# Ten pairs of token tiles in seven block products instead of eight, in the second projection of an attention-and-MLP kernel

## The chip, the cores and the metric

The kernel runs on one core of a Trainium2 chip. A core has five engines with instruction queues of their own: TensorE (PE: matrix products, into PSUM), VectorE (DVE), ScalarE (ACT: activations and copies), GpSimd (POOL), and SyncE (SP), which here only issues DMAs. They meet through semaphores. SBUF is the working memory; PSUM has eight banks of 512 fp32 columns, into which TensorE accumulates and which VectorE and ScalarE read. The metric is device time in microseconds, the median of the runs.

## The reference

Four batches of eight heads, 768 positions, head size 64; every query sees the first four positions and a window of 128. The attention output, as 3072 tokens of 512 features, goes through two projections with a gate between them.

```python
scores = q @ k^T / sqrt(64)          # keep: position < 4, or 0 <= row - column < 128
a = softmax(where(keep, scores, -1e9))
x = (a @ v) as (3072, 512)
h = x @ w_in                         # (512, 2048)
g = h * (1 / (1 + exp(-beta * h)))   # beta: one number per column
out = g @ w_out                      # (2048, 512), fp32
```

## The kernel before

**Blocks.** The tokens are cut into eight blocks of 384 (half a batch each; `hb` in the attention part, `T_` in the projections). A block is three token tiles of 128. For each block the kernel loads q, k and v (`load`, 256 KB each, into fp32 staging buffers `stg`, two slots per name), casts them to bf16 (`cast`), brings q and k into a transposed layout (`T` on TensorE for blocks 0 to 2, `XP` with DMA transposes issued by SyncE from block 3, `CUT`, on), computes scores in bursts of up to three tiles (`SC`, `band`, `SS`), takes exponentials on ScalarE, masks on GpSimd and VectorE, multiplies by v (`AV`), normalises on VectorE and transposes the result into `xT` (`OT`, again DMA transposes from block 3 on).

**First projection.** `HQ(T_, m)` makes one of the sixteen groups of 128 hidden features of a block: four 384-column matmuls (line 1023) into one bank, a tanh on ScalarE (line 1028), and `(t + 1) * h` on VectorE (line 1030) into `g`, bf16. That is twice the gated value, so a factor 0.5 is left for the output. There are three `g` buffers.

**Second projection.** `OQ(T_, t, j)` is a quarter of one token tile: four matmuls with a 128x128 piece of `g` as the stationary operand and 512 columns of `w_out16` as the moving one (line 1046). After the fourth quarter the bank is copied to `osb` with the factor 0.5 (`copies`, on ScalarE line 524 or VectorE line 530) and stored (line 1064). The very last tile is done in two parts of 384 and 128 columns.

**Who sets the order.** Nothing loops at run time. `later` is a string, written out by hand, of one letter per step (T, S, A, R, H, O); each letter takes the next step of its kind. `background` puts loads, casts and DMA transposes in between by their estimated times. Every operation is recorded in `Graph` with its reads and writes; `any_of` gives a choice of engines. `arrange` then orders the operations of every engine by estimated ready times (it may move a group of matmuls a few places) and keeps GpSimd and some VectorE operations apart (`lock`). Each engine runs its list in order; `resolve` turns dependences into semaphore waits.

Of the kernel before, what the change touches and what calls it, by code (L numbers as in the profile page):

```python
# [4 lines left out]
BF16 = mybir.dt.bfloat16  # L5
# [22 lines left out]
class Graph:  # L28
# [15 lines left out]
    def __init__(self):  # L44
        self.ops = []
        self.writers = {}
        self.readers = {}
        self.last_x = {}
        self.free = {e: 800.0 for e in self.ENGINES}
        self.dma_free = 2500.0  # L50
        self.stalls = [(16000.0, 1100.0), (34000.0, 700.0)]
        self.port = {"gp": 0.0, "dve": 0.0}
        self.group = 0
        self.filler, self.fill_to = None, 0
# [5 lines left out]
    def add(self, eng, fn, ns=0, r=(), w=(), x=(), dma=None, alts=None, after=(), hold=550, chain=None, lock=False):  # L60
# [31 lines left out]
        at = self.free[eng]  # L92
        for p, _ in deps:
            at = max(at, p.end + (0 if p.eng == eng and not p.dma else self.HOP))
        self.place(o, at)
        self.ops.append(o)
        return o

# [296 lines left out]

def _program(nc, G, sb, ps, q, k, v, w_in, w_out, beta, out):
# [49 lines left out]
    BAND, KW = 8, 64  # L446
    LANES, QUADS = [6,7], [3,5,7]
# [5 lines left out]
    def any_of(alts, r=(), w=(), x=(), lock=False):  # L453

        return G.add(min(alts, key=lambda e: G.free[e] + alts[e][1]), None, 0, r, w, x, None, alts, lock=lock)
# [134 lines left out]

    def load(hb, n, i):

        b, t0, z = hb // 2, hb % 2 * HALF, hb % NSTG
# [10 lines left out]
        after = [("stg", n, z, j) for j in range(4)] if hb in range(CUT, CUT + NSTG) and n != "v" else ()  # L604
# [20 lines left out]
    def cast_w(j):  # L625
# [13 lines left out]
        any_of(copies(dst, src_, {"act": 947} if j in W0 else {"gp": 1060} if j < 4 else {"act": 947, "dve": 602, "gp": 1060}), r=[("wst", j % NWS)], w=[("w16", m, h)], lock=True)  # L639

    def cast(hb, n, i):

        z = hb % NSTG
# [371 lines left out]
    def HQ(T_, m):  # L1015
# [6 lines left out]
        for c in range(4):  # L1022
# [4 lines left out]
        spare_ = [("wst", NWS // 2 + z) for z in range(NWS // 2)] if (T_, m) == (NG - 1, 0) else []  # L1027
        add("act", lambda e: e.activation(tt[ti][:, :], hp, AF.Tanh, bias=0.0, scale=hbeta[:, m:m + 1]),  # L1028
            act_ns(HALF) + 93, r=["hbeta"], w=[("t", ti)], x=[("B", bs[0])])
        add("dve", lambda e: e.scalar_tensor_tensor(gt[T_ % NG][:, m, :], tt[ti][:, :], 1.0, hp, ALU.add, ALU.mult),  # L1030
            dve_ns(HALF), r=[("t", ti)], w=[("g", T_, m)] + spare_, x=[("B", bs[0])])
# [5 lines left out]
    def OQ(T_, t, j):  # L1037
# [7 lines left out]
        for m in range(4 * j, 4 * j + 4):  # L1045
# [3 lines left out]
                r=[("w16", 4 + m // 4, m // 2 % 2), ("g", T_, m)], x=[("B", bk)])  # L1049
        if j == 3 and n < NOUT:  # L1050
            z = os_i[0] % NOS
            os_i[0] += 1
            add("act", lambda e: e.activation(osb[z][:, 0:n], P[:, bk, 0:n], AF.Copy, bias=0.0, scale=0.5),
# [4 lines left out]
        elif j == 3:  # L1058
            z = os_i[0] % NOS
            os_i[0] += 1  # L1060
            any_of(copies(osb[z][:, :], P[:, bk, :], {"dve": 608, "act": 493}, 0.5), w=[("osb", z)], x=[("B", bk)])
# [6 lines left out]


# [15 lines left out]
    OS += [(T_, t, j) for T_ in range(1, NSB) for t in range(3) for j in range(4 + 4 * ((T_, t) == (NSB - 1, NK - 1)))]  # L1085
    XPS = [(hb, n, c) for hb in range(CUT, NSB) for n in "qk" for c in range(NK)]
    n_cast, n_w, n_x = [0], [0], [0]
    BACKLOG, AHEAD, MARGIN = 6000, 300, 200

    def head(s):  # L1090
# [50 lines left out]
        elif s == "H":  # L1141
# [3 lines left out]
            if done["O"] < 12 * (T_ - NG + 1) or T_ == NG - 1 and n_w[0] < 16:  # L1145
                return None
# [3 lines left out]
        else:  # L1150
# [3 lines left out]
            t = G.at([("g", T_, m) for m in range(j % 4 * 4, j % 4 * 4 + 4)] + [("w16", 4 + j % 4, 0), ("w16", 4 + j % 4, 1)])  # L1154
# [9 lines left out]
    def background():  # L1164
# [3 lines left out]
        while moved:  # L1168
            moved = False
            i = done["load"]  # L1170
            if i < len(LOADS) and G.dma_free <= now + BACKLOG:
# [12 lines left out]
                elif x[0] - NSTG < at_hb:  # L1184
                    load(*x)
                    mark(("in",) + x, ("stb" if x[1] == "v" or x[0] >= CUT else "stg", x[1], x[0] % NSTG, x[2] or 0))
# [12 lines left out]
            if n_x[0] < len(XPS):  # L1199
                hb, n, c = XPS[n_x[0]]  # L1200
                if n_cast[0] > CASTS.index(XPS[n_x[0]]) and units_scored() >= 4 * (hb - NT // 4 + 2):
# [6 lines left out]
            if n_w[0] < 16:  # L1208
                t = G.at([("win", n_w[0])])
                if t is not None and t <= now + AHEAD:  # L1210
                    cast_w(n_w[0])
                    n_w[0] += 1
                    moved = True

# [67 lines left out]
    for x in early:  # L1282
# [5 lines left out]
        if x[0] == "T":  # L1288
# [6 lines left out]
    later = ("AAAAHOORORORROHHHHHHHHHHTTOTOOSTOOOOSOSOHHAAHAAHRHHRRORHOOOSOOOOSHOOHHHHARHRRRHHHHOHHHHOHO"  # L1295
             "OOOSOOOOSOOHHHARARAHRHHHHARHOOHHHHHHHOOOSOOOOSOHHHHOHHOHHHHHHAHHHHRRROOOOOSOROSOOOOARAARRA"
# [51 lines left out]
```

## Time and profile before

| | |
|---|---|
| median of 3 runs | 220.45 us (219.76 to 220.48) |
| span of the profiled execution | 218.1 us (the runs include some 2.3 us more around it) |
| TensorE busy, granted clock | 213.7 us (98%), 1.000 |
| VectorE, ScalarE, GpSimd busy | 133.1, 149.9, 73.3 us |
| first projection on the chain that ended last | 31% of the span |
| second projection on that chain | 36% of the span |
| moved by DMA | 39.88 MB, mean 183 GB/s |

How to read it: the busy time of an engine is a share of the span, and idle time of an engine that nobody waits for costs nothing. The chain that ended last is followed back from the last instruction through whatever released each step; its entries give the spacing of matmuls, while the duration of a single matmul overlaps its neighbours. A row of groups gives the line, engine, operation, tile out and in, shapes, count, then busy time and mean nanoseconds of one, then the idle time before it and what ended that. `SPq` rows are DMAs being issued by SyncE.

### The profile page before, as it was taken

Reading aid. Unit: us, or ns where it says so; the run is one execution under the profiler, and the core shown is the slowest. Engines: PE = TensorE matmul, PEld = TensorE weight load, DVE = VectorE, ACT = ScalarE, POOL = GpSimd, SP = SyncE. Lnnn points to the kernel's source line nnn. Section 1 sums busy time; section 2 is a strip of 40 time slices with the busy share of each in tenths; the row PEclk is TensorE's granted clock in tenths of the full one; section 3 lists DMA queues with packets and bytes.
Section 4 is the critical chain, followed back from the end, with each engine's and each line's share of the span. In section 5 each row is a group of like instructions: output and inputs, shape, how many; then the busy total and the mean of one; then the engine's idle time right before and its main releaser. Section 6 shows DMA issues by size and latency. Waiting matters only on the chain.

```text
span 218.1 us, 4823 instructions
## 1 busy us (share of the span) xinstructions
PE 213.7 (98%) x1915; PEld 119.5 (55%) x1915; DVE 133.1 (61%) x290; ACT 149.9 (69%) x246; POOL 73.3 (34%) x138
## 2 busy tenths in 40 slices
PE   8999999999999999999999999999999999999995
PEld 3556557555475465446554556447565465455443
DVE  1786999697884378446960479368885266086100
ACT  2798998586875986559777895386896683287221
POOL 8215551112540874055205670162021970100100
PEclk9999999999999999999999999999999999999999
DMA  6999999999979999699966999969758113300122
GB/s 194 255 326 370 351 281 315 379 304 215 198 178 151 221 152 223 159 206 220 165 148 156 207 244 158 186 160 213 146 91 184 45 61 92 114 2 0 51 96 96
DMA packets 94718, 39.88 MB, mean 183 GB/s; under 512 B 82072, under 2 KB 89512, under 8 KB 94696
## 3 DMA queue, kind: packets, MB, share of 16 engines
q1 hardware_dynamic: 91928, 33.28, 71.1%
q0 software_dynamic: 1680, 5.51, 7.8%
q10 hardware_dynamic: 1088, 0.79, 1.1%
q8 instruction: 15, 0.25, 0.5%
q14 instruction: 7, 0.06, 0.1%
HBM read 27.37 MB, written 6.29 MB: 154 GB/s over the span
## 4 chain that ended last, share of the span: by engine, by line
PE 76%; DMA 10%; SPq 7%; DVE 3%; ACT 2%; issue 1%
PE P L1046 36%; PE P L1023 31%; DMA k_stage<-in_k_dram 5%; DMA g<-in_moe_w_in_dram 5%; SPq L605 4%; PE P L979 4%; PE P L830 3%; SPq L617 2%; DVE g L1030 1%; DVE E L911 1%; PE P L726 1%; SPq L1257 1%; PE P L923 1%; ACT t L1028 1%; ACT E L892 0%
## 5 line engine op out<-in xcount | busy, mean ns | idle before, releaser
L1028 ACT ACTIVATE t<-P,hbeta 128x384 f32<-128x384 f32 x128 | 72.3, 587 | 25.4 <-PE P L1023 19.2
L1023 PE MATMUL P<-xT,w_in 128*128 128x384 bf16 x512 | 88.7, 326 | 0.4 <-DVE g L1030 0.2
L1046 PE MATMUL P<-w_out,g 128*128 128x512 bf16 (+2 forms) x400 | 89.0, 371 | 0.0
L1030 DVE SCALAR_TENSOR_TENSOR g<-t,P 128x384 bf16<-128x384 f32 x128 | 67.9, 551 | 26.9 <-ACT t L1028 22.1
L1023 PEld LDWEIGHTS P<-xT,w_in 128*128 128x128 bf16 x512 | 48.9, 98 | 34.3 <-DVE g L1030 0.9
L1046 PEld LDWEIGHTS P<-w_out,g 128*128 128x128 bf16 x400 | 37.2, 98 | 40.0 <-issue 0.7
L892 ACT ACTIVATE E<-P 128x1024 bf16<-128x1024 f32 x44 | 43.3, 1035 | 10.4 <-PE P L830 10.0
L907 POOL TENSOR_SCALAR_AFFINE_SELECT E<-E 128x512 bf16<-128x512 bf16 x57 | 37.6, 686 | 29.4 <-ACT E L892 29.3
L1064 POOL DMA_DIRECT2D out_dram<-osb x21 | 11.8, 563 | 57.4 <-ACT osb L524 57.4
L524 ACT ACTIVATE osb<-P 128x512 f32<-128x512 f32 x15 | 9.0, 598 | 18.7 <-PE P L1046 18.6
L985 DVE TENSOR_TENSOR onorm<-P,rden 128x384 bf16<-128x384 f32 x32 | 17.7, 554 | 0.9
L529 DVE CAST vaug<-v_stage 128x512 bf16<-128x512 f32 x18 | 8.8, 489 | 13.8 <-DMA v_stage<-in_v_dram 13.8
L979 PE MATMUL P<-vaug,E 128*128 128x65 bf16 x352 | 14.4, 193 | 0.0
L979 PEld LDWEIGHTS P<-vaug,E 128*128 128x128 bf16 x352 | 13.6, 97 | 1.4
L901 DVE TENSOR_TENSOR E<-E,maskS 128x512 bf16<-128x512 bf16 x16 | 7.4, 476 | 8.6 <-ACT E L892 8.6
L1266 PE MATMUL P<-const-bfloat16-1.0 128*128 128x512 bf16 (+1 forms) x37 | 11.7, 444 | 0.8 <-PEq L1330 0.8
L526 POOL TENSOR_SCALAR_AFFINE_SELECT q<-q_stage 128x512 bf16<-128x512 f32 x8 | 5.3, 657 | 20.4 <-DMA q_stage<-in_q_dram 20.4
L530 DVE TENSOR_SCALAR osb<-P 128x512 f32<-128x512 f32 x8 | 5.5, 689 | 7.9 <-PE P L1046 7.9
L524 ACT ACTIVATE k<-k_stage 128x512 bf16<-128x512 f32 (+1 forms) x16 | 9.6, 612 | 0.4 <-DMA k_stage<-in_k_dram 0.4
L830 PEld LDWEIGHTS P<-qkT 64*64 64x64 bf16 x336 | 6.2, 107 | 5.5 <-issue 4.7
L830 PE MATMUL P<-qkT 64*64 64x192 bf16 (+3 forms) x336 | 8.5, 233 | 0.0
L524 ACT ACTIVATE qkT<-P 128x384 bf16<-128x384 bf16 (+1 forms) x10 | 5.2, 553 | 4.4 <-PE P L726 4.3
(66 smaller groups left out, 116.8 us busy)
## 6 DMA issues: line engine op xcount, KB each, us to landing
v_stage<-in_v_dram SPq DMA_DIRECT2D x24, 256.0 KB, 5.0
out_dram<-osb POOLq DMA_DIRECT2D x21, 256.0 KB, 2.9
q_stage<-in_q_dram SPq DMA_DIRECT2D x15, 256.0 KB, 5.1
k_stage<-in_k_dram SPq DMA_DIRECT2D x15, 256.0 KB, 4.8
wst<-in_moe_w_in_dram SPq DMA_DIRECT2D x5, 512.0 KB, 8.2
wst<-in_moe_w_out_dram SPq DMA_DIRECT2D x4, 512.0 KB, 8.7
g<-in_moe_w_out_dram SPq DMA_DIRECT2D x4, 512.0 KB, 7.5
q_stage<-in_q_dram SPq DMA_DIRECT2D x2, 768.0 KB, 8.0
```

What stands on the lines that cost most here:

```text
L524: return lambda e: e.activation(dst, src, AF.Copy, bias=0.0, scale=scale)
L830: e.matmul(P[KW * c:KW * c + KW, bk, 128 * i0 + a:128 * i0 + z_], qkT[rows, own_ % NT, 1, kc + KW * c:kc + KW * c + KW], qkT[rows, u % NT, ...
L892: add("act", lambda e, src=src, dst_=dst_: e.activation(dst_, src, AF.Exp, bias=0.0, scale=SCALE), act_ns(1024), w=[("E", z)] + [("m", z, ...
L907: alts = {"gp": (lambda e, dd=dd, sg=sg: e.affine_select(dd, dd, [[0, n] for n in dd.shape[1:-1]] + [[sg, 128]], ALU.is_ge, 0.0, base=min( ...
L979: e.matmul(A[:, c0:c0 + D + 1], E[t_ % NE][:, i, hh, :], vaug[vz][:, kb % NK, 2 * hp + hh, :], start=a, stop=o, skip_group_check=True), 31,
L985: add("dve", lambda e: e.tensor_tensor(onorm[on][:, :, :, :].rearrange("p m h d -> p (m h) d"), av[:, :, 0:D], rden[on][:, :].unsqueeze(2) ...
L1023: add("pe", lambda e, c=c: e.matmul(hp, w_in16[:, c, m * 128:(m + 1) * 128], xT[:, c, t0:t0 + HALF], start=(c == 0), stop=(c == 3)), mm_ns ...
L1028: add("act", lambda e: e.activation(tt[ti][:, :], hp, AF.Tanh, bias=0.0, scale=hbeta[:, m:m + 1]), act_ns(HALF) + 93, r=["hbeta"], w=[("t" ...
L1030: add("dve", lambda e: e.scalar_tensor_tensor(gt[T_ % NG][:, m, :], tt[ti][:, :], 1.0, hp, ALU.add, ALU.mult), dve_ns(HALF), r=[("t", ti)] ...
L1046: add("pe", lambda e, m=m: e.matmul(P[:, bk, 0:n], gt[T_ % NG][:, m, t * 128:(t + 1) * 128], w_out16[:, m, cols], start=(m == 0), stop=(m ...
L1064: add(eng, lambda e: e.dma_start(out_t[3 * T_ + t], osb[z][:, :]), 262144 / 300, r=[("osb", z)], dma=f"do{eng}{z}", hold={"sp": 550, "gp": ...
L1266: G.fill([lambda e, n=n: e.matmul(P[:, 7, 0:128 * n], one.to_broadcast([128, 128]), one.to_broadcast([128, 128 * n]), start=True, stop=Tru ...
```

## The change

Token tiles are taken in pairs: tiles 0 and 1 of each of the blocks 1 to 7, and tile 2 of blocks 1 and 2, 3 and 4, 5 and 6 together (`PAIRS_OF`). Block 0 and the last tile are computed as before. For a pair, `g` is a 2 x 2 matrix of blocks A (two token tiles; even and odd hidden groups, eight each), and `w_out` a 2 x 2 matrix B (even and odd hidden groups; left and right 256 columns). In place of eight block products the kernel forms seven, in the Winograd form of Strassen's scheme:

- On the operand side, per pair: S1 = A21 + A22, S2 = S1 - A11, A11 - A21 (over A21 in `g`), and A12 - S2 (over A12 in `g`, after product 2). Once for all: four combinations of w_out's blocks (`w_sums`, `Tw`).
- Each product (`WP`) is eight matmuls of 256 columns. The order is 1, 6, 2, 7, 5, 4, 3. Products 2, 7 and 3 accumulate onto the banks of 1, 6 and 5 after those have been read.
- On the output side, products 1 and 2 are copied out, and five additions on VectorE combine a bank with an SBUF tile (`plus`). Two tiles are then stored.

The sums live in the second slot of the q, k and v staging buffers and in three of the `w_out` staging buffers. So blocks from 3 on load into slot 0 alone, and a load waits for the cast of the block before it. The factor 0.5 moves into the casts of `w_out`, which go to ScalarE or VectorE. The planner may put an operation into an earlier gap of an engine while it records (`place_early`), g's dependences are kept per token tile, and `later` is a new string.

```diff
+    def place_early(self, o, eng):
+        if eng in ("pe", "sp") or o.dma:
+            self.place(o, max(self.free[eng], self.ready_at(o, eng)))
+            return
...
+def PAIRS_OF():
+    own = {T_: ((T_, 0), (T_, 1)) for T_ in range(1, NSB)}
+    out_ = []
+    for T_ in range(1, NSB):
+        out_.append(own[T_])
+        if T_ % 2 == 0:
+            out_.append(((T_ - 1, 2), (T_, 2)))
+    return out_
...
+    def slot(hb):
+        return hb % NSTG if hb < CUT else 0
...
-        b, t0, z = hb // 2, hb % 2 * HALF, hb % NSTG
+        b, t0, z = hb // 2, hb % 2 * HALF, slot(hb)
...
+        else:
+            any_of(copies(dst, src_, {"act": 947, "dve": 602}, 0.5), r=[("wst", j % NWS)], w=[("w16", m, h)], lock=True)
...
+    Tw = [flat[n][:, 0:8 * HN].rearrange("p (i f) -> p i f", f=HN) for n in "qkv"]
+    Tw.append(wf[0].bitcast(BF16)[:, 0:8 * HN].rearrange("p (i f) -> p i f", f=HN))
+    Sb = [flat[n][:, 8 * HN:8 * HN + 1024] for n in "qkv"] + [wf[1].bitcast(BF16)[:, 0:1024]]
...
+    PROD = (1, 6, 2, 7, 5, 4, 3)
+    def w_sums():
...
+            for n, x, y, r in ((0, hi_[:, ev, :], lo[:, ev, :], []),
+                               (1, hi_[:, od, :], Tw[0][:, at, :], [("T", 0, a)]),
+                               (2, hi_[:, od, :], hi_[:, ev, :], []),
+                               (3, lo[:, od, :], Tw[1][:, at, :], [("T", 1, a)])):
...
+    def s_op(d, x, y, op, r, w, after=()):
+        fn = lambda e: e.tensor_tensor(d, x, y, op)
+        c = 8 // NA * 128
+        any_of({"dve": (fn, c / 1.92 + 67), "gp": (fn, 2.17 * c + 80)}, r=r, w=w, lock=True, after=after)
+    def sums(n, a):
...
+        s_op(s1, g_of(n, 2, a), g_of(n, 3, a), ALU.add, g_keys(n, 2, a) + g_keys(n, 3, a), [("S", z, 1, a)], was)
+        s_op(s2, s1, g_of(n, 0, a), ALU.subtract, g_keys(n, 0, a) + [("S", z, 1, a)], [("S", z, 2, a)], was)
+        s_op(g_of(n, 2, a), g_of(n, 0, a), g_of(n, 2, a), ALU.subtract, g_keys(n, 0, a) + g_keys(n, 2, a),
+             g_keys(n, 2, a))
...
+    def last_sum(n, a):
...
+        s_op(g_of(n, 1, a), g_of(n, 1, a), Sb[2 * z + 1][:, at, :], ALU.subtract, g_keys(n, 1, a) + [("S", z, 2, a)],
+             g_keys(n, 1, a))
...
+    def operands(n, p):
...
+        return {1: (g_of(n, 0), g_keys(n, 0), lo[:, ev, :], allw), 2: (g_of(n, 1), g_keys(n, 1), lo[:, od, :], allw),
+                3: (g_of(n, 1), sk(4), hi_[:, od, :], allw), 4: (g_of(n, 3), g_keys(n, 3), Tw[3], tk(3)),
+                5: (Sb[2 * z], sk(1), Tw[0], tk(0)), 6: (Sb[2 * z + 1], sk(2), Tw[1], tk(1)),
+                7: (g_of(n, 2), sk(3), Tw[2], tk(2))}[p]
...
+    def WP(n, k):
+        G.begin()
+        p, z = PROD[k], n % 2
...
+        for i in range(8):
+            add("pe", lambda e, i=i: e.matmul(P[:, bk, 0:HN], lhs[:, i, :], rhs[:, i, :],
+                                              start=p in (1, 6, 5, 4) and i == 0, stop=i == 7, skip_group_check=True),
+                mm_ns(HN), r=keys if i in (0, 7) else (), x=[("B", bk)])
...
+        def plus(d, u, r, w, after=()):
+            add("dve", lambda e: e.tensor_tensor(d, src, u, ALU.add), 310, r=r, w=w, x=[("B", bk)], after=after)
+        if p == 1:
+            any_of(copies(s1, src, {"dve": 310, "act": 285}), r=[], w=[S1], x=[("B", bk)], after=was)
+        elif p == 6:
+            plus(u2, s1, [S1], [U2], was)
+        elif p == 2:
+            any_of(copies(oa[:, 0:HN], src, {"dve": 310, "act": 285}), w=[ka], x=[("B", bk)])
+            for a in range(NA):
+                last_sum(n, a)
+        elif p == 7:
+            plus(u3, s1, [S1], [U3], was)
...
+            plus(ob[:, HN:NOUT], u3, [U3], [kb])
...
+            plus(ob[:, 0:HN], u3, [U3], [kb + (1,)], [kb])
...
+            plus(oa[:, HN:NOUT], u2, [U2], [ka + (1,)], [ka])
...
-    OS += [(T_, t, j) for T_ in range(1, NSB) for t in range(3) for j in range(4 + 4 * ((T_, t) == (NSB - 1, NK - 1)))]
+    OS += [(None, n, k) for n in range(len(PAIRS)) for k in range(len(PROD))]
+    OS += [(NSB - 1, NK - 1, j) for j in range(8)]
...
-    later = ("AAAAHOORORORROHHHHHHHHHHTTOTOOSTOOOOSOSOHHAAHAAHRHHRRORHOOOSOOOOSHOOHHHHARHRRRHHHHOHHHHOHO"
+    later = ("AAAAHOOROORRROHHHHHOHHHHHTTOOTOSTOOOSSHHAHAAHARHHOROORRHOOSOOSHHHHHHHHARHHRHRHRHHHOSOOSOOO"
...
```

More of the change, by code (lines that the diff above doesn't have):

```diff
@@ new lines, in last_sum, with sums_when @@
+    def last_sum(n, a):
+        z = n % 2
+        at = slice(8 // NA * a, 8 // NA * (a + 1))
+        s_op(g_of(n, 1, a), g_of(n, 1, a), Sb[2 * z + 1][:, at, :], ALU.subtract, g_keys(n, 1, a) + [("S", z, 2, a)],
+             g_keys(n, 1, a))
+        mark(("Su", n, 4, a), g_keys(n, 1, a)[0])
+    n_sum = [0]
+    def sums_when(T_, m):
+        while n_sum[0] < NA * len(PAIRS):
+            n, a = divmod(n_sum[0], NA)
+            if n >= 2 and pairs_done[0] < n - 1:
+                return
+            if any(k not in G.writers for w_ in (0, 2, 3) for k in g_keys(n, w_, a)):
+                return
+            sums(n, a)
+            n_sum[0] += 1
@@ L1309, in _program @@
             G.free["pe"] = now + 200
-            assert now < 260000, (done, s)
+            assert now < 500000, (done, s)
         if s == "SC":
```

160 lines of the change are left out of this document (139 added, 21 removed).

## The prediction, made before the changed kernel had run

> **What bounds the kernel now.** I read the page first (span and busy time), then the busy time by stretches, then the chain that ended last in order of time.
>
> ```profile
> span 218.1 us, 4823 instructions
> PE 213.7 (98%) x1915; PEld 119.5 (55%) x1915; DVE 133.1 (61%) x290; ACT 149.9 (69%) x246; POOL 73.3 (34%) x138
> ...
> 60.00:80.00 20.00, 20.00 (x222) 11.46 (x221) 11.32 (x26) 16.51 (x28) 10.64 (x17) 1.00 1.08 181
> ...
> 180.00:200.00 20.00, 20.00 (x126) 10.92 (x123) 11.14 (x24) 11.09 (x19) 1.08 (x2) 1.00 0.19 55
> ```
>
> The columns of the stretches are PE, PEld, DVE, ACT, POOL busy, then granted clock, DMA share and GB/s. From 60 to 200 us TensorE is busy in all of each of the seven stretches of 20 us (the first and the last are shown), at clock 1.00: it is the bound, with no stall to win back. A change pays by taking work off TensorE, and loses whatever new waits it puts into TensorE's order. The profiled execution spans 218.1 us; the runs have a median of 220.45, so some 2.3 us lie around the span, and I carry them over unchanged.
>
> The chain gives the true spacing of matmuls (the mean of one overlaps its neighbours):
>
> ```profile
> 131.82 0.28 PE P L952 x12
> 132.10 1.56 PE P L979 x48
> ...
> 149.47 14.95 PE P L1023 x92
> ...
> 182.70 6.91 PE P L1046 x32
> ```
>
> A 512-column matmul costs 6.91/32 = 215.9 ns, a 384-column one 162.5 ns, a 65-column one 32.5 ns. The first two differ by 53.4 ns for 128 columns, which is 2.4 columns a ns; at that pace the three are the column time plus 2.6, 2.5 and 5.4 ns. All of these load 128x128 weights of their own, so a 256-column matmul must cost 106.7 plus 2.6 to 5.4: 109.3 to 112.1 ns.
>
> **The saving.** A pair of token tiles was 32 matmuls of 215.9 ns, 6.91 us; it becomes 7 products of 8 matmuls of 256 columns: 56 x 109.3 = 6.12 us (6.28 at 112.1). Over ten pairs TensorE loses 7.9 us (6.3 at the other bound). I take 7.9, since the longer matmuls are the nearer rows. Tile block 0 and the last tile stay as they were, and so does the tail of the kernel (two part matmul groups, eviction, store): 0.
>
> On this place a rule speaks against the change. The Trainium skill, "TensorE: Matmul & The Clock Gate", section "Back-to-back issue gap", gives a sustained spacing of about 81 ns at 128 columns and 131 ns at 512, so nearly a fixed cost per matmul. By it, an estimate for 256 columns on the line between them is 98 ns, the pair would go from 4.2 to 5.5 us, and ten pairs would cost 13 us. The trace disagrees: 215.9 ns at 512.
>
> **What it adds to VectorE.** Four sums of 128x1024 bf16 a pair (38 of the 40 stand on VectorE in the changed kernel's order, 2 on GpSimd), eight weight sums (5 on VectorE, 3 on GpSimd), five additions from PSUM of 256 columns a pair, and two plain evictions of 256 in place of two of 512.
>
> ```profile
> L901 DVE TENSOR_TENSOR E<-E,maskS x16: 406/422/860, 9.7 to 146.0; 128x512 bf16<-128x512 bf16 x16
> ...
> L985 DVE TENSOR_TENSOR onorm<-P,rden 128x384 bf16<-128x384 f32 x32 | 17.7, 554 | 0.9
> ...
> L983 DVE RECIPROCAL rden<-P 128x6 f32<-128x6 f32 x32 | 5.8, 185 | 1.3 <-PE P L979 1.3
> ...
> 44.48 0.69 DVE L529 CAST w_out<-g 128x1024 bf16<-128x1024 f32 x1
> 45.08 1.48 DVE L1030 SCALAR_TENSOR_TENSOR g<-t,P 128x384 bf16<-128x384 f32 x3
> ```
>
> No 1024-wide two-input operation is in this trace. From below: a cast of 1024 takes 0.69 us and the next instruction starts 0.60 after it; a two-input bf16 operation of 512 takes 0.42, about the pace of that cast. From above: the pace of PSUM reads, (554-185)/378 = 0.98 ns an element, makes 1024 take 1.18 us. I take 0.69 (spacing 0.61), because the mask row is the same operation at half the width. A PSUM addition of 256 is 185 + 250 x 0.98 = 0.43 us (spacing some 0.36). VectorE's sum: 43 x 0.61 + 50 x 0.36 = 44 us more, less 8 evictions of 512 at 185 + 506 x 0.98 = 0.68 (spacing 0.6); copies added and casts gone to ScalarE about cancel. So about 39 more: 172 of 210 us. As a total it still fits under TensorE; what counts is the places where TensorE waits for it.
>
> GpSimd gets five two-input operations of 1024.
>
> ```profile
> L526 POOL TENSOR_SCALAR_AFFINE_SELECT w_in<-wst 128x1024 bf16<-128x1024 f32 x4 | 4.2, 1052 | 4.1 <-DMA wst<-in_moe_w_in_dram 4.1
> ...
> L698 POOL TENSOR_TENSOR kS<-qkT,headm 128x32 bf16<-128x32 bf16 x2 | 0.5, 240 | 1.6 <-DMA qkT<-k 1.5
> ```
>
> These rows bound one: 0.24 us (128x32, the same operation) from below; twice the 1.05 us of a one-input 128x1024 cast, 2.1, from above. I take 2.1. Three of these are weight sums at about 43 to 50 us, one on VectorE waits for one of them while TensorE runs block 0's second projection: 0, and up to 1.5 us if that cover were gone. On ScalarE evictions of 256 columns take the place of ones of 512, and some ten more casts come; the output factor 0.5 moves into the casts of w_out, which GpSimd no longer takes. ScalarE is busy 69% and stays beside TensorE: 0.
>
> **Where TensorE must now wait.** The sums of an own pair (tiles 0 and 1 of a block) read all sixteen g tiles of the block, so they start after the block's last first-projection group.
>
> ```profile
> 202.81 0.65 PE P L1023 x4
> ...
> 203.50 0.58 ACT L1028 ACTIVATE t<-P,hbeta 128x384 f32<-128x384 f32 x1 [1.78 <-PE P L1023]
> 204.11 0.55 DVE L1030 SCALAR_TENSOR_TENSOR g<-t,P 128x384 bf16<-128x384 f32 x1 [3.55 <-ACT t L1028]
> ```
>
> The group ends at 203.46 and ScalarE starts 0.04 later; g is done at 204.66: 1.20 us. S1, and S2 which reads S1, each after a wait of the same 0.04: 2 x 0.73. To TensorE 0.04 again. Product 6 can start 2.7 us after the group's end. Inside a pair, three products accumulate into a bank that VectorE or ScalarE must read first; that takes 0.04 + 0.43 + 0.04 = 0.51 us, and one product in between covers 0.87, if VectorE is free. I went through the changed kernel's order for what TensorE has in between (a product of eight matmuls 0.87, a score burst 0.7, four attention units 0.28 + 1.56, three transposes 3 x 56 ns = 0.17):
> - Pair 0 (block 1): two products and two sets of transposes, 2.1: wait 0.6. Product 7 then waits for the addition after product 6, which stands behind two sums on VectorE (1.22 us, then 0.43 and 0.04), while product 6 and transposes cover 1.04: another 0.65.
> - Pair 1 (block 2): product 1 and a score burst, 1.6: wait 1.1. Product 7, behind two sums and a mask: 0.3.
> - Pair 3 (block 3): two products, a score burst and the sink scores, about 2.6 of cover: wait 0.1; product 7, behind sums and a copy, 0.3.
> - Pair 4 (block 4): four attention units and product 1, 2.7: no wait, but the four units' normalisations now stand behind the sums and hold four banks, which the next score burst needs: 0.9.
> - Pairs 6, 7 and 9 (blocks 5 to 7) have 3.5 us or more: 0, and 0.25 in pair 7. Pairs 2, 5 and 8 use g tiles of a block before: 0.
>
> Together 4.2 us.
>
> **The staging buffers.** Blocks from 3 on now load into one slot, so a load waits for the cast of the block before it. The rows that bear on it, of the cast, of SyncE's queue and of the score bursts:
>
> ```profile
> 59.92 0.41 DVE L529 CAST q<-q_stage 128x512 bf16<-128x512 f32 x1
> ...
> 63.88 1.64 SPq L709 DMA_TRANSPOSE qkT<-k  x1
> 65.56 3.13 SPq L605 DMA_DIRECT2D v_stage<-in_v_dram  x3
> 68.74 3.44 SPq L605 DMA_DIRECT2D k_stage<-in_k_dram  x3
> ...
> 160.59 3.89 SPq L709 DMA_TRANSPOSE qkT<-q  x3
> ...
> 69.51 0.70 PE L830 MATMUL P<-qkT 64*64 64x192 bf16 x32
> ...
> 167.59 0.70 PE L830 MATMUL P<-qkT 64*64 64x192 bf16 x32
> ```
>
> The row of one of block 3's last casts (59.92) stands 9 us ahead of block 4's loads (68.74), so the slot itself costs 0 unless casts slip by more than that. From the end of block 3's transposes (65.5) to that of block 7's (164.5) SyncE takes 99.0 us; in the new order one load (3.44/3 = 1.1) and four transposes (1.3 each, 3.89/3) move out of that stretch: 92.7. TensorE's work from block 3's score burst to block 7's is 98.1 now (69.5 to 167.6), and 88.4 in the new order, counted with the same rows: 63 first-projection groups of 0.65 stand between them in place of 72, and the rest is the shorter products. So block 7's scores need some 4.3 us of waits in that stretch if SyncE's queue gains nothing; the joints above already put 4.2 us there, mostly in the same places, and the two do not add. I add 0.8 us for what does not overlap (block 6's x transposes now stand behind block 7's). In all 5.0 us of new waits: 218.1 - 7.9 + 5.0 = 215.2 of span, and 220.45 - 2.9 = 217.5.
>
> **Rivals.**
> - *The cover is better than I count* (all joints hidden but 1 us): 213.5. For it: VectorE was idle 85 us, and the interleaved pairs need no wait at all. Against: pairs 0 and 1 have too little between by the order itself.
> - *VectorE's queue decides, slower.* Its instructions run in order, and each bank-emptying addition that stands behind a sum, a cast that waits for a load, or a normalisation delays a product. Twenty such accumulating products remain beside the joints; at 0.35 us each (half a sum) they cost 7 us: 217.5 + 7.0 - 1.9 (joints that fall into them) = 222.6. It decides from 0.15 us each on, where the whole gain is gone. For it: from block 2's last first-projection group to block 3's fourth I count 13.8 us of VectorE work beside 12.3 us of TensorE work. Against: in most pairs first-projection groups stand between, and VectorE has idle time there.
> - *Sums at the slow pace*, 1.18 us: S1 and S2 add 1.0 us at pairs 0, 1, 3 and 4, so 221.5; against it the mask row.
> - *The change does not save matmul time*: with a fixed cost of 35 ns a matmul the 24 more per pair eat all of it, and with the 5 us of waits it is 225. The 32.5 ns of a whole 65-column matmul all but exclude it. The skill's rule above is this rival, and would give 233.
>
> For contention I quote the Trainium skill, "SBUF — State Buffer", section "Who interferes with whom": a VectorE instruction with two SBUF inputs blocks a GpSimd instruction that reads SBUF, and the reverse. The mask row's 860 against 422 agrees. GpSimd is 34% busy, so I price it 0.
>
> **How the numbers follow.** Forecast 0.48 (its own range 215 to 220; 0.08 of it within 0.5%), better cover 0.20, VectorE's queue 0.22 (0.05 within 0.5%), slow sums 0.07 (half within), no saving 0.03. Faster than 219.35 (0.5%, about what a measurement of this kernel can tell): 0.40 + 0.20 = 0.60. Within 0.5%: 0.16. Slower: 0.24. The range runs from the better cover, 213.5, to 222, which leaves out about half of the slower cases.
>
> **What would show it.** Right: TensorE's chain shows 256-column products at 109 ns (0.87 us for eight); TensorE waits for VectorE's sums at the ends of blocks 1 and 2; VectorE busy near 172 us; PE's busy time falls by about 8 us while the span falls by 3. Wrong: eight products above 0.95 us; score bursts waiting for transposes by more than 2 us; additions late in every pair; a sum above 1 us.

## The result, and the profile after

The changed kernel takes 222.87 us (median; 221.55 to 223.73) against 220.34 of the kernel before: ratio 1.0125, 95% interval 1.0082 to 1.0167. It is slower by 1.25%; 217.5 us was predicted. The profiled execution is the one of 221.55 us. Here and below a median is over all runs, while a ratio leaves out the runs that took over 1.5% more than the fastest of the same kernel.

The page of the changed kernel, with the shares of its last chain by engine; the last line is that of the kernel before:

```profile
span 219.8 us, 5396 instructions
PE 209.0 (95%) x2155; PEld 141.5 (64%) x2155; DVE 173.8 (79%) x375; ACT 152.8 (70%) x261; POOL 82.7 (38%) x136
...
PE 54%; DVE 20%; DMA 10%; SPq 7%; ACT 6%; issue 2%
...
PE 76%; DMA 10%; SPq 7%; DVE 3%; ACT 2%; issue 1%
```

TensorE's busy time fell by 4.7 us while the span grew by 1.7. On the chain that ended last TensorE holds 54% in place of 76%; VectorE's share grew from 3% to 20% and ScalarE's from 2% to 6%, while those of DMAs and SyncE's queue stayed. The busy time by stretches (columns as in the prediction's fence):

```profile
60.00:80.00 20.00, 18.06 (x223) 12.54 (x223) 12.76 (x29) 15.52 (x28) 9.97 (x17) 1.00 1.15 179
160.00:180.00 20.00, 19.53 (x246) 13.98 (x245) 14.73 (x35) 13.19 (x22) 11.05 (x15) 1.00 0.46 105
180.00:200.00 20.00, 19.93 (x152) 14.57 (x151) 16.16 (x33) 10.99 (x21) 2.17 (x4) 1.00 0.22 68
```

Where TensorE had no gap from 60 to 200 us, it now has 1.9 us of gaps in 60 to 80, 0.5 in 160 to 180 and almost none from 180 to 200. The chain's last row of products, and the groups of the new operations (busy, mean ns of one, idle before):

```profile
205.11 8.73 PE P L1245 x80
```

```profile
L1253 DVE TENSOR_TENSOR osb<-P,wst 128x256 f32<-128x256 f32 x30 | 12.2, 417 | 3.7 <-PE P L1245 3.5
...
L1167 DVE TENSOR_TENSOR g<-g 128x1024 bf16<-128x1024 bf16 x9 | 6.6, 731 | 0.0
...
L1167 DVE TENSOR_TENSOR q_stage<-g 128x1024 bf16<-128x1024 bf16 x5 | 3.4, 686 | 0.1
...
L1167 POOL TENSOR_TENSOR g<-g 128x1024 bf16<-128x1024 bf16 x1 | 2.6, 2627 | 4.8 <-DVE q_stage L1167 4.8
...
L1150 POOL TENSOR_TENSOR q_stage<-w_out 128x1024 bf16<-128x1024 bf16 x2 | 4.3, 2130 | 9.8 <-DVE w_out L577 9.8
```

The prices are close to the forecast: 8.73/80 = 109.1 ns a product matmul, 0.68 to 0.76 us a sum in the mean of a group (0.73 over all 38 on VectorE, 0.69 forecast), 0.42 an addition, 2.13 to 2.63 a sum on GpSimd (2.1 forecast), and VectorE at 173.8 us (172).

So the loss is in waits. I added up, for every matmul, its start less the start of the one before, less the spacing that its kind has in an unbroken run (215.9, 162.5, 109.1, 32.5 ns and so on). What is left over is waiting:

| us from the first matmul | 0-40 | 40-60 | 60-80 | 80-120 | 120-160 | from 160 | all |
|---|---|---|---|---|---|---|---|
| before | 4.9 | 1.1 | -0.3 | 0.4 | -0.2 | -0.3 | 5.6 |
| after | 5.1 | 2.3 | 3.1 | 3.4 | 0.6 | 0.9 | 15.3 |

9.7 us more waiting against a span that is 1.7 longer gives 8.0 us of saved matmul time. The saving came as forecast (7.9), the new waits are twice what was forecast (5.0). They are many and short. By the same kind of count, from 40 us on, the waits ahead of second-projection matmuls grew from 1.6 to 6.2 us and those ahead of first-projection groups from 0.2 to 2.8. The longest entries of TensorE's waits (weight loads, since they wait first; total, times, longest), and behind the dots two rows of the kernel before:

```profile
PEld P L1078 <- DVE g L1086: 3.4, 7, 1.0
...
PEld P L1245 <- DVE g L1086: 2.4, 4, 1.2
...
PEld P L1060 <- DVE onorm L1040: 1.8, 4, 0.6
PEld P L930 <- DVE qkT L576: 1.4, 1, 1.4
PEld P L781 <- DVE k L576: 1.3, 3, 0.8
PEld P L1245 <- DVE wst L1253: 1.3, 4, 0.5
...
PEld P L1005 <- DVE onorm L985: 1.2, 3, 0.4
...
PEld P L1023 <- DVE g L1030: 0.9, 3, 0.5
```

The wait of L930 stands at 8 us, in the start-up. A first-projection group (L1078) reads no g; when it waits for g's operation, it waits for the bank that this operation empties.

### The profile page after: what moved, and what is told of

The parts are those of the page before. It is cut to its first block, busy times and chain, and to the rows that moved or that the text cites. A ratio compares the mean times of both kernels' runs of the same rounds, so it can differ in the third digit from the quotient of the medians.

```text
span 219.8 us, 5396 instructions
## 1 busy us (share of the span) xinstructions
PE 209.0 (95%) x2155; PEld 141.5 (64%) x2155; DVE 173.8 (79%) x375; ACT 152.8 (70%) x261; POOL 82.7 (38%) x136
## 4 chain that ended last, share of the span: by engine, by line
PE 54%; DVE 20%; DMA 10%; SPq 7%; ACT 6%; issue 2%
PE P L1245 22%; PE P L1078 22%; DVE g L1086 9%; SPq L656 5%; DMA g<-in_moe_w_in_dram 4%; DMA g<-in_moe_w_out_dram 4%; PE P L1102 4%; PE P L1034 3%; ACT t L1084 3%; ACT E L947 2%; DMA v_stage<-in_v_dram 2%; PE P L885 2%; DVE g L1167 1%; DVE onorm L1040 1%; SPq L668 1%
## 5 line engine op out<-in xcount | busy, mean ns | idle before, releaser
L1078 PE MATMUL P<-xT,w_in 128*128 128x384 bf16 x512 | 91.3, 326 | 2.0 <-DVE g L1086 0.8
L1078 PEld LDWEIGHTS P<-xT,w_in 128*128 128x128 bf16 x512 | 48.4, 98 | 33.9 <-DVE g L1086 3.4
L1245 PE MATMUL P<-w_out,g 128*128 128x256 bf16 x240 | 30.7, 273 | 1.4 <-DVE g L1086 1.1
L1245 PEld LDWEIGHTS P<-w_out,g 128*128 128x128 bf16 x240 | 22.7, 98 | 6.1 <-DVE g L1086 1.8
L1102 PE MATMUL P<-w_out,g 128*128 128x512 bf16 (+2 forms) x80 | 15.3, 337 | 0.0
L1253 DVE TENSOR_TENSOR osb<-P,wst 128x256 f32<-128x256 f32 x30 | 12.2, 417 | 3.7 <-PE P L1245 3.5
L1245 PE MATMUL P<-v_stage,g 128*128 128x256 bf16 x80 | 10.4, 273 | 0.4 <-DVE wst L1253 0.4
L1253 DVE TENSOR_TENSOR wst<-P,wst 128x256 f32<-128x256 f32 x20 | 8.3, 417 | 2.8 <-PE P L1245 2.8
L1245 PE MATMUL P<-wst,g 128*128 128x256 bf16 x80 | 10.4, 273 | 0.0
L1102 PEld LDWEIGHTS P<-w_out,g 128*128 128x128 bf16 x80 | 6.9, 98 | 5.2
L571 ACT ACTIVATE k<-k_stage 128x512 bf16<-128x512 f32 (+1 forms) x12 | 7.4, 616 | 3.7 <-DMA k_stage<-in_k_dram 3.7
L571 ACT ACTIVATE wst<-P 128x256 f32<-128x256 f32 x9 | 3.4, 383 | 8.1 <-PE P L1245 8.0
```

The source lines that it names most:

```text
L1078: add("pe", lambda e, c=c: e.matmul(hp, w_in16[:, c, m * 128:(m + 1) * 128], xT[:, c, t0:t0 + HALF], start=(c == 0), stop=(c == 3)), mm_ns ...
L1102: add("pe", lambda e, m=m: e.matmul(P[:, bk, 0:n], gt[T_ % NG][:, m, t * 128:(t + 1) * 128], w_out16[:, m, cols], start=(m == 0), stop=(m ...
L1245: add("pe", lambda e, i=i: e.matmul(P[:, bk, 0:HN], lhs[:, i, :], rhs[:, i, :], start=p in (1, 6, 5, 4) and i == 0, stop=i == 7, skip_grou ...
L1253: add("dve", lambda e: e.tensor_tensor(d, src, u, ALU.add), 310, r=r, w=w, x=[("B", bk)], after=after)
```

## The experiments

Ratios are against the kernel before on the same chip. The code cuts are abridged. In the runs e1 to e12, but for e8, the planner plans every operation as in the changed kernel (in e10: as in the kernel before), and only then the named ones are dropped or untied, so the order on each engine stays what it was. What waited for a dropped operation waits for what that one waited for:

```diff
-        self.ops = new
+        flat = lambda o, ds: [x for p, raw in ds for x in (flat(o, p.deps) if p.skip else [(p, raw)])]
+        self.ops = [o for o in new if not o.skip]
...
+            o.deps = flat(o, o.deps)
```

**Are the sums the cause?** Four runs: the operand sums dropped (e1); run, but with no reader (e2); the weight sums dropped (e3); both kinds dropped (e4).

```diff
 # e1, in s_op
+        G.skip = True
         any_of({"dve": (fn, c / 1.92 + 67), "gp": ...}, r=r, w=w, lock=True, after=after)
+        G.skip = False
-                5: (Sb[2 * z], sk(1), Tw[0], tk(0)), 6: (Sb[2 * z + 1], sk(2), Tw[1], tk(1)),
+                5: (g_of(n, 3), sk(1), Tw[0], tk(0)), 6: (g_of(n, 1), sk(2), Tw[1], tk(1)),
 # e2: G.apart in place of G.skip: the sums stay, a product that waited for one waits for its inputs;
 #     the sums over g write to Sb[2 * z + 1]; a sum also waits for the sum before it
 # e3, in w_sums: G.skip around any_of, and in operands:
+        Tw = [lo[:, ev, :], lo[:, od, :], hi_[:, ev, :], hi_[:, od, :]]
 # e4: e1 and e3
```

> The 40 operand sums (four a pair) are left out: products 5 and 6 read the odd k tiles of the pair's second and first tile instead, and 3 and 7 read tiles that were not changed, so the output is not the reference's. Everything else stands in the order of the changed kernel on each engine, and the products still wait for the g tiles. The changed kernel waits 9.7 us more on TensorE than the kernel before and saves 7.9. If the sums are the cause (as results that products wait for, or as work on VectorE), the 4.2 us of new waits ahead of products go and some of those ahead of first-projection groups: 215 to 218 us. If the single staging slot or the additions out of PSUM are the cause, it stays above 220.

> The 40 operand sums run where they ran, on the same engines and in the same order, but write to scratch, and the products read tiles of g as in the run without sums, so no product waits for a sum; the output is not the reference's. If the waits are for the sums' results (the joints of the prediction), this is within 1 us of the run without sums, 215 to 218. If the waits come from the time that the sums take on VectorE ahead of other work (the rival of VectorE's queue), it stays within 1.5 us of the changed kernel: 221 to 223.

> The eight sums of weights are left out, products 4 to 7 read plain quarters of w_out, so the output is not the reference's; the order of the rest is that of the changed kernel. Priced 0 in the prediction, since block 0's second projection covers them: then 222.9 as before. If they delay the casts and transposes of block 2 through VectorE and the port shared with GpSimd (some 1.3 us of new waits stand at 40 to 60 us, 3.4 at 60 to 80): 220 to 221.5.

> Both kinds of sums are left out (as in the two runs that leave out one); the products, their additions, the one staging slot and the order of the rest stay; the output is not the reference's. If the sums make all 9.7 us of new waits: 213 to 214. What it stands above 213.5 is the share of the slot, the additions out of PSUM and the new order: if the slot binds (SyncE's queue, priced 0.8 beyond the joints), 217 or more.

Measured: e1 222.04 us, ratio 1.0087 (1.0056 to 1.0117); e2 223.19, 1.0113 (1.0058 to 1.0169); e3 221.99, 1.0086 (1.0056 to 1.0117); e4 221.45, 1.0045 (1.0009 to 1.0081). My expectation of e1, 215 to 218, was missed by far. Without any sum (e4) the kernel gains 0.8% on the changed one (1.0125 to 1.0045; 1.8 us, uncertain by some 1.2); what either kind alone brings lies within the uncertainty. The kernel is still not faster than the one before. In e4's profiled execution the waits add up to 13.4 us, 1.9 less than in after. So the sums, as results that products wait for (the joints) or as work on VectorE ahead of other work, take 1.8 of the 8.0 us that were to be won, and most of the loss lies elsewhere.

**Are products waiting for g, or for the emptying of their banks?** Three runs on e4's base: products that wait for no g (e5), products whose banks nobody has to empty (e6), and both (e7).

```diff
 # e5: in the flattening above, dependences of a product on g's operation are cut; the weights are old
-        lhs, _, rhs, _ = operands(n, p)
+        lhs, _, rhs, _ = w_out16[:, 0:8, 256:384], *operands(n, p)[1:]
 # e6: the two copies and five additions of a pair read SBUF, and TensorE's waits for them are cut
-        src = P[:, bk, 0:HN]
+        src = hbeta[:, 0:1].to_broadcast([128, HN])
```

> The run without sums, and in it the products do not wait for any g tile either: their weights are a slice of w_out that is long there, so the output is not the reference's. The order on each engine is that of the changed kernel. The run without sums stands at 221.5 us and shows 4.6 us of waits ahead of products on TensorE. If those are for the g tiles of the last first-projection groups of a block (the whole chain of the joints less the sums): 217.5 to 219. If they are for the emptying of banks, or the waits only move on to the next work: 220.5 or more.

> The run without sums, and in it the five additions and two copies of a pair run where they ran, on the same engines, but read an old SBUF tile and not PSUM, so no TensorE work waits for them to empty a bank; the output is not the reference's. The order is that of the changed kernel. If the products' banks (up to three held at once, each emptied by VectorE or ScalarE in their queues' order) are the cause of the waits that are left: 217.5 to 219. If it is the g tiles: 220.5 or more.

> The two edits together on the run without sums: products wait neither for g nor for a bank of a product; the output is not the reference's. What stays is 7.9 us less matmul time and the new order of the groups, the single staging slot, and first-projection groups that wait for their own banks. If products and their banks are the whole loss: 213.5 to 214.5. Whatever it stands above that is the share of the order, the slot and the transfers.

Measured: e5 222.12 us, 1.0068 (1.0033 to 1.0103); e6 221.72, 1.0094 (1.0065 to 1.0122); e7 221.92, 1.0098 (1.0070 to 1.0126). No gain in any of them, where e7 was to give 214 if products were the loss. e6 and e7 have a price of their own: an addition that reads SBUF took 0.47 to 0.53 us in the mean of a group, against 0.42 in e4, 4 to 5 us of VectorE in all; e5 has no such price. The waits only changed places. TensorE's waits of e7:

```profile
PE P L1078 <- DMA xT<-onorm: 1.7, 2, 1.5
PE P L1245 <- DVE g L1087: 1.4, 2, 1.1
PE P L885 <- DMA qkT<-k: 1.4, 1, 1.4
PE P L1078 <- ACT E L947: 0.9, 2, 0.7
...
PE P L1078 <- DVE g L1087: 0.8, 2, 0.6
```

First-projection groups now wait 1.7 us for the DMA transposes of onorm and a score burst 1.4 for those of k: SyncE's queue, the bound that by the prediction does not add to the joints. The products that wait for g's operation here read no g: they take over a bank from a first-projection group.

**Is it SyncE's queue?** Its issues in the changed kernel, in one stretch (start, time):

```profile
139.03 5.09 SPq L1054 DMA_TRANSPOSE xT<-onorm  x4
144.16 0.67 SPq L720 DMA_DIRECT2D vS<-in_v_dram  x1
144.87 0.46 SPq L656 DMA_DIRECT2D k_stage<-in_k_dram  x1
145.38 2.85 SPq L656 DMA_DIRECT2D q_stage<-in_q_dram  x2
148.27 2.01 SPq L656 DMA_DIRECT2D k_stage<-in_k_dram  x2
```

One issue follows another. From 56 to 170 us the queue is issuing in 101.5 of 114 us (105.3 in the kernel before). Four runs: the kernel before with the single slot alone (e8), and the 20 transposes of onorm left out of the changed kernel (e9), of the kernel before (e10) and of e7 (e11).

```diff
 # e8, on the kernel before; the load conditions as in the change
-        b, t0, z = hb // 2, hb % 2 * HALF, hb % NSTG
+        b, t0, z = hb // 2, hb % 2 * HALF, slot(hb)
 # e9, e10, e11, in OT and HQ
+            G.skip = True
             add("sp", lambda e: e.dma_start_transpose(dst, src), 750, ...
-        t0 = T_ % NXT * HALF
+        t0 = T_ % (3 if T_ >= CUT else NXT) * HALF
```

> The kernel before with the single staging slot alone: blocks from 3 on load into slot 0, each load after the casts of the block before; TensorE's order is that of the kernel before, nothing is left out. If the slot makes loads and transposes late (the rival for which the prediction counted 4.3 us at SyncE's queue): 221.5 to 224. If it is hidden: 220.1, within 0.5%.

> The changed kernel, sums and all, without the 20 DMA transposes of onorm into xT (blocks 3 to 7); first-projection groups of those blocks read the xT of blocks 0 to 2, so the output is not the reference's. Order as in the changed kernel. SyncE's queue is without a gap from 56 to 170 us, and with products that wait for nothing the transfers were still waited for. If TensorE, with 7.9 us less work, runs into that queue, taking 20 x 1.3 us out of it wins most of the loss: 215 to 218. If the waits are those of VectorE and ScalarE (banks, g tiles, normalisations): 221 or more.

> The same edit on the kernel before (20 transposes out, output not the reference's). Its TensorE had no wait from 60 us on, so if the queue only just kept up with it: 219 to 220.3, no more than 0.5% faster.

> The run without sums whose products wait neither for g nor for a bank, and now also without the 20 transposes; the output is not the reference's. If products and transfers together are the loss: 213 to 215. What stands above 213.5 is first-projection groups, scores and attention units that wait for VectorE and ScalarE through their own banks.

Measured: e8 219.83 us, 0.9997 (0.9974 to 1.0020); e9 221.16, 1.0060 (1.0031 to 1.0089); e10 220.24, 1.0010 (0.9977 to 1.0042); e11 217.61, 0.9907 (0.9876 to 0.9938). The slot is free of cost, as priced. The kernel before gains nothing from a shorter queue, the changed one 0.65% (1.4 us, uncertain by some 1.1), and e7 1.9% (4.2 us). So e9 lies where I expected it if VectorE and ScalarE were the cause, and e11 lies above its 213 to 215. That is the pattern of bounds that lie behind one another: with the products' waits there, the queue is mostly hidden; with these gone, the queue takes what they took. The edit leaves out the transposes as well as their place in the queue, so a group's wait for xT goes either way. But 1.4 us of e7's waits are those of a score burst at 91.2 us for k's transposes, which e11 keeps, and there e11 does not wait. That 4.2 us is near the prediction's 4.3 for the queue is in part chance: the 4.3 was for block 7's scores, and e7's waits for transposes stand at 91, 148 and 169 us and not there.

e11 is still 5.6 us above what the matmul time alone would give (220.0 - 8.0 = 212.0). One run asks whether this is the banks of the first-projection groups.

```diff
 # e12, on e11: tanh and g's operation read SBUF, TensorE's waits for them are cut
-            act_ns(HALF) + 93, r=["hbeta"], w=[("t", ti)], x=[("B", bs[0])])   # input hp, the bank
+            ...                                                                 # input hbeta, broadcast
```

> The run without sums, product waits and transposes (217.6 us), and in it the tanh and the g operation of every first-projection group read an old SBUF tile instead of PSUM, so that no TensorE work waits for ScalarE or VectorE to empty a bank of such a group; both still run, in the same order; the output is not the reference's. 5.8 us of waits are left there beside the start-up's 5.6, most of them at 59 to 114 us, put down to VectorE's g and ScalarE's E. If it is the banks of the first-projection groups: 213.5 to 215. If it is the attention's chain (scores, exponentials, normalisations): 216.5 or more.

Measured: 219.13 us, 0.9951 (0.9912 to 0.9991), above the 213.5 to 215 expected if it is the groups' banks, and no gain over e11. TensorE's longest waits in e12, and the masks on GpSimd in e11 and in e12:

```profile
PE P L885 <- DMA qkT<-k: 2.2, 2, 1.6
PE P L1034 <- POOL E L962: 1.9, 1, 1.9
PE P L930 <- DVE qkT L576: 1.5, 1, 1.5
PE P L1023 <- ACT E L947: 1.2, 1, 1.2
```

```profile
L962 POOL TENSOR_SCALAR_AFFINE_SELECT E<-E 128x512 bf16<-128x512 bf16 x57 | 40.3, 736 | 30.7 <-ACT E L947 30.7
...
L962 POOL TENSOR_SCALAR_AFFINE_SELECT E<-E 128x512 bf16<-128x512 bf16 x57 | 46.6, 846 | 29.9 <-ACT E L947 29.9
```

This run tells less than was asked of it. The last three of these waits stand at 39.9, 8.7 and 35.9 us: by 40 us the profiled e12 is 4.0 us behind e11, and from there to the end it gains 1.0. The edit also made others slower: a mask takes 846 ns in place of 736, and the operation for g 623 in place of 550. Behind 40 us the groups' waits for their banks went, and the longest wait that came is that of a score burst at 93.3 us for k's transposes, so for SyncE's queue again. Whether the attention's chain is the last of the bounds, as 216.5 or more was to mean, no run isolates, and what makes up the 5.6 us stays open.

**The order of the groups.** Four runs compute all of it. In c1 the sums go in halves and each matmul waits for its own operands only. In c4, c2 and c3 the letters of `later` were moved about until the planner's own costs liked them better; c4 keeps ten pairs, c2 has pairs from block 3 on, c3 from block 5 on.

```diff
 # c1
-    NA = 1
+    NA = 2
-                mm_ns(HN), r=keys if i in (0, 7) else (), x=[("B", bk)])
+                mm_ns(HN), r=fine_keys(n, p, i), x=[("B", bk)])
 # c4: later alone. c2 (from 3) and c3 (from 5), and later:
-    for T_ in range(1, NSB):
+    for T_ in range(3, NSB):
-    OS += [(None, n, k) for n in range(len(PAIRS)) for k in range(len(PROD))]
+    OS += [(T_, t, j) for T_ in range(1, 3) for t in range(NK) for j in range(4)] + [(None, n, k) ...]
```

> The changed kernel with nothing left out, its operand sums in two halves each (k tiles 0 to 7 and 8 to 15), and each matmul of a product waiting only for its own g tile, half sum and half weight sum instead of all at the first. The halves can start before the last first-projection groups of a block. If the joints are a good part of the loss: 220.5 to 221.5. If another bound stands right behind them: 222 to 223.5 (VectorE has 40 more instructions).

> Nothing left out. Blocks 0 to 2 with the old second projection, seven products for the seven pairs of blocks 3 to 7 alone, and an order of the groups set anew (the kernel before's up to block 2, then a changed one). The saving is 7 x 0.79 = 5.5 us. The changed kernel's new waits by region are 6.2 us at 40 to 100 us, where these blocks now stand as in the kernel before, and 3.3 behind. If the waits belong to the early blocks (weight sums, transfers still at full rate, first joints): 217.5 to 219. If any shortening of TensorE's work before SyncE's queue ends near 165 us is eaten: 219.5 to 221.

> Nothing left out. Seven products for the four pairs of blocks 5 to 7 alone, the old second projection for blocks 0 to 4, the order set anew. The saving is 4 x 0.79 = 3.2 us, nearly all behind the last score burst, where SyncE's queue no longer matters and the changed kernel shows almost no new wait. If that is where the scheme pays: 217 to 218.5. If the single banks and joints eat it there too: 219.5 to 221.

> Nothing left out. The changed kernel with its ten pairs of seven products, only the order of TensorE's groups after the first 15 first-projection groups is another, chosen so that banks and g tiles are ready sooner with additions out of PSUM at the 0.42 us of the trace. If the order is a good part of the loss: 219 to 221. If the bounds lie in the engines and the queue whatever the order: 222 to 223.5.

Measured: c1 254.60 us, 1.1494 (1.1426 to 1.1561); c4 228.15, 1.0387 (1.0341 to 1.0434); c2 222.78, 1.0129 (1.0103 to 1.0156); c3 223.10, 1.0141 (1.0115 to 1.0168). All slower, and each above both of its expected ranges, c1 by far. The timeline of c1 shows how:

```profile
173.96 1.46 PE L1078 MATMUL P<-xT,w_in 128*128 128x384 bf16 x4 [1.26 <-DVE g L1086]
...
175.46 0.58 ACT L1084 ACTIVATE t<-P,hbeta 128x384 f32<-128x384 f32 x1 [2.14 <-PE P L1078]
176.07 0.55 DVE L1086 SCALAR_TENSOR_TENSOR g<-t,P 128x384 bf16<-128x384 f32 x1 [2.17 <-ACT t L1084]
176.68 0.13 PEld L1078 LDWEIGHTS P<-xT,w_in 128*128 128x128 bf16 x2 [1.95 <-DVE g L1086]
176.68 1.46 PE L1078 MATMUL P<-xT,w_in 128*128 128x384 bf16 x4 [1.26 <-DVE g L1086]
```

One first-projection group after another waits for the g operation of the one before, 2.7 us each in place of 0.65 (2.1 before the clock fell, see the end): they share one bank. An open pair of products holds up to two banks from its first to its last matmul, a score burst needs neighbouring free ones, and the planner gave the groups what was left. The bank numbers themselves are not in the profile; that the groups wait for g's operation, which they do not read, shows it. In c3 the waits lie where its products begin, 17.5 us of TensorE work in 20:

```profile
160.00:180.00 20.00, 17.54 (x223) 11.54 (x222) 13.38 (x28) 11.69 (x17) 8.68 (x14) 1.00 0.41 99
```

c2 and c3 moved letters of early blocks too, so they don't tell whether the scheme can pay. Nor does any run compute the old quarters in the changed kernel's order and with its `place_early`, so how much of the loss is the new order alone isn't known; c4, which differs from the changed kernel in the letters of `later` only, shows that it can be 5 us. The last two runs are made on e8: TensorE's order is that of the kernel before up to the place of the first pair, `place_early` is not used, the weight sums run late and on VectorE, the factor 0.5 is applied by the additions, and no score burst or first-projection group stands inside a pair, but for one burst in c6.

```diff
 # c5 (pairs: own pairs of blocks 6 and 7), on the kernel before with one slot; c6 has block 5's too
+            if done["SC"] >= WHEN and not w_sum:
+                w_sum.append(w_sums())
 # later, behind the last S
-    "HOOHHHHARRRORHHOOOOOOOOHHHHHHHHHHHHHHHOOOOHOOOOOOOOOOOOOOOOOO"
+    "HOOHHHHARRRORHHOOOOOOOOOHHHHHHHHHHHHHHHHOOOOOOOOOOOOOOOOOOO"
```

> Nothing left out. The kernel before with one staging slot; TensorE's order is its own up to the last score burst. Behind it the two own pairs of blocks 6 and 7 are done in seven products each, with two or more quarters of the old form or 2.6 us of other work between a block's last first-projection group and product 6, and no score burst or first-projection group inside a pair; the weight sums run on VectorE alone, after block 4's first g tile. If shortening TensorE's work pays where no transfer, score or attention unit follows, and costs nothing ahead of it: 2 x 0.79 = 1.6 us less, 218.2 to 219.0. If the scheme's banks and sums eat it there too: 220 to 221.

> Nothing left out. As the kernel with the last two pairs, and block 5's own pair in seven products too; these stand between the last two score bursts, one burst inside the pair, so the first of the two bursts comes a product later and 0.8 us less work stands ahead of block 7's attention. If only what lies behind the last score burst pays, it is no faster than the kernel with two pairs, 218.3 to 219.5; if every pair pays there: 217.4 to 218.2.

Measured: c5 218.75 us, 0.9914 (0.9884 to 0.9944): 0.9% faster than the kernel before, 2.1% faster than the changed one (0.9914/1.0125), and as expected. c6 219.44, 0.9953 (0.9921 to 0.9985): the third pair brings nothing. c5's busy time by stretches and its chain's row of the last pair:

```profile
60.00:160.00 100.00, 100.00 (x967) 57.16 (x966) 67.25 (x147) 74.06 (x124) 37.51 (x62) 1.00 0.97 181
160.00:180.00 20.00, 20.00 (x179) 10.62 (x177) 10.86 (x20) 15.15 (x24) 10.64 (x18) 1.00 0.45 100
```

```profile
205.77 6.11 PE P L1200 x56
```

The profiled execution is c5's slowest, 219.59 us; against the one of the kernel before it lost 1.1 us in the first 60 us, where nothing is changed. TensorE has no gap from 60 to 180 us, and 56 product matmuls take 6.11 us where 32 of the old ones took 6.91. In c6, by the sum of waits, 1.0 us is waited in 160 to 180 us, where c5 has none. Its third pair saves 0.8. So behind the last score burst the scheme pays all or most of the 1.6 us that two pairs save (1.5 by the medians; 1.3 from 60 us on, between the two profiled executions), and one pair ahead of it, with a burst inside, does not.

## Why the prediction was wrong

- *Matmul cost and saving*: right. 109.1 ns against 109.3 forecast, and 8.0 us against 7.9. The fixed-cost rival, with the Trainium skill's sustained spacing of matmuls ("TensorE: Matmul & The Clock Gate", section "Back-to-back issue gap"), fell with it: 256 columns cost 109.1 ns, 512 cost 215.9.
- *Prices of sums and additions, and VectorE's total*: right to 6% on VectorE; on GpSimd the bound of 2.1 us from above did not hold (2.13 to 2.63). "Sums at the slow pace" fell with them.
- *The single slot at no cost*: right (e8, 0.9997).
- *Weight sums at 0*: not refuted alone (e3), but both kinds of sums together cost 1.8 us and waits at 40 to 60 us grew by 1.2.
- *"In all 5.0 us of new waits"*: this is the step that failed. It was 9.7. Ahead of products the waits grew by 4.6 us, close to the 4.2 of the joints; ahead of first-projection groups they grew by 2.6, for which the sum had only the 0.8 of block 6's x transposes; the rest, 2.5 us, stands ahead of transposes and attention work. The joints were placed where waits are found, at the ends of blocks 1 to 3, but the sums were the smaller part of them: without any sum 13.4 of 15.3 us of waits stay (e4), and with products that wait neither for g nor for their own banks the kernel is no faster (e7). So the new waits are not a list of joints that add up.
- *The reason under it* was the first paragraph's: TensorE has no stall, so work taken off it pays. That holds only as far as the others could go faster. The chain of the kernel before showed who ended last, and not how close behind the next ones were. Taking TensorE's time away brought up SyncE's queue (4.2 us, e7 to e11); what holds the 5.6 us behind that stays open. The waits for the products' banks, which ScalarE and VectorE empty, could be taken away without any gain (e6, with slower additions); those of the groups' banks were worth some 1 us behind 40 us (e12, with slower neighbours).
- *"The joints above already put 4.2 us there", and "the two do not add"*: right, and I did not draw the consequence. If they don't add, then hiding the joints wins nothing while the queue stands. The rival "better cover" at 213.5 was thus not to be had; e7, with all cover, gives 221.9.
- *The rival of VectorE's queue* gives 222.6 and the result is 222.9, which is luck, since the mechanism is another: it put the loss on the sums and additions ahead of each other, and dropping the sums (e1), or freeing what the additions hold up (e6), brings back 0.8 us at most.
- *Signs*: eight matmuls of a product in 0.87 us, VectorE near 172, and waits at the ends of blocks 1 and 2 were seen. TensorE's busy time fell by 4.7 and not by 8; a product's matmul is shown with 273 ns in the mean against a spacing of 109, so part of a wait lies under the matmul before it and counts as busy.

## What to carry to other kernels

An engine that is busy 98% of the time is the bound only by as much as the next chain is slack: before work is taken off it, take the work of each neighbour away in a run (or price it over the same stretch), since a saving of 8 us is worth little when the DMA queue takes 4 of it back (e7 to e11) and other waits the rest. Shorten the bound engine first where nothing else is left to do, here behind the last score burst, where two pairs won 1.5 us and ten pairs lost 2.5. When something is left out for a test, leave the order of all the rest as it was: a new order alone moved the time by 5 us (c4). And look at what the edit does to the neighbours' times before reading the result (e6, e12).

## What the runs showed of the hardware

- In c1, in a stretch where TensorE worked for about half of the time (10.4 of 20 us from 160 on) and had no gap longer than 1.8 us, its granted clock fell, to 0.54 in the mean from 170 to 185 us. In the page's row of the 40 slices:

```profile
PEclk9999999999999999999999999997556999999999
```

  and four 384-column matmuls took 1.46 us there in place of 0.82. A wait can so make the work behind it dearer; in after the clock stayed at 1.00.
- A GpSimd sum of 128x1024 took 2.13 to 2.29 us, and 2.63 in one case; VectorE's took 0.68 to 0.76 in the mean of a group.
